# Seven block products for the last two chunk pairs of the first row group, in a linear-attention and bilinear feed-forward kernel

## The chip, the cores and the metric

The kernel runs on one core of a Trainium2 chip. The metric is the device time of one execution in microseconds. The kernel before takes 216.21 us, the median of three runs (216.19 to 216.22). The profiled execution has a span of 215.1 us; all times of single instructions below are from its start.

## The reference

Two stages, the second on the rows of the first:

```python
# attention with decay, per head, in blocks of 64 rows
intra = (q_b @ k_b.T * Dmask) @ v_b          # Dmask: lam**(i-j) for i >= j
inter = (q_b * lam**(pos+1)) @ kv_state
out_b = intra + inter
kv_state = lam**64 * kv_state + (k_b * lam**(63-pos)).T @ v_b
# bilinear feed-forward: x is (3072, 512), w_a and w_b (512, 1536), w_out (1536, 512)
out = ((x @ w_a) * (x @ w_b)) @ w_out
```

There are 4 batches, 8 heads, 768 rows a batch and 64 columns a head, so x has 512 columns. Inputs and output are float32.

## The kernel before

A **unit** is 128 rows of one batch; there are 24, and the kernel takes them in seven groups of 4, 2, 4, 4, 4, 4 and 2 units (`GROUPS`). For each unit q and k are multiplied by powers of lam (`make_qs`, `make_ks`, both L276), transposed (on TensorE by `piece_T` for units 4 to 7, by a DMA for units 8 to 23), multiplied into scores and masked (`piece_S`: TensorE L344, VectorE L361), and a running state is updated (`piece_V`). `pieces_O` makes the attention output of one or two units, transposed, as the tile xT of the group, and calls `sums`, which forms four sums and differences of xT's quarters (xs, L573 to L576).

The feed-forward part of a group follows. The 1536 inner columns are 12 chunks of 128, or 6 pairs. There are two ways to do it:

- **Directly**, in the first group (`ffn` with first set). For each chunk four matmuls make a (L518), ScalarE copies it, four make b, and VectorE multiplies the two from PSUM into ab (L545).
- **By seven block products**, in groups 1 to 6 (`ffn_seven`). x, and w_a and w_b side by side, are cut in 2 x 2 blocks, and seven products of blocks stand in for eight. The weights' sums are made once: `w_sums(i)` makes the tile tw of pair i by four VectorE subtractions (L548 to L551), t0 from the first halves of w_a and w_b, t1 and t3 also from the second. A pair takes the products in the order 1, 5, 2, 6, 3, 7, 4, mixed with those of the next pair. Product 1, then 6, 7 and 4, add up in one PSUM bank, m_q; 5 and 3 share m_r; 2 has m_p. Between them ScalarE copies s1, s5 and u2 out, and VectorE (or GpSimd) forms c11, c12 and c22 (L629 or L632, L640, L646). Product 4 adds into m_q only after VectorE has read it for c22. Two multiplications write ab: c22 by m_q on VectorE (L649), c11 by c12 on GpSimd (L642).

The output is ab @ w_out. In the first group it runs over the four units of a pair of chunks at a time (L833, `out_mms`), with other work between: after each chunk and each piece of the output a `hook(slot)` runs what `PLAN` lists for that group and slot. The slots of the first group are 0 to 11 for the chunks and 12 to 35 for the 24 pieces of the output. Groups 2 to 5 use seven block products for the output too, which need sums of w_out (`wo_sums(j)`, the tiles two, same lines as tw).

In `PLAN`, TW is w_sums, TO is wo_sums, T a transpose on TensorE, S scores and mask, V the state, O2 the attention output of two units, L loads, P both scalings of a unit, QS that of q on GpSimd, KS that of k on VectorE. Each engine works its instructions in program order, so the place in PLAN is the place in every engine's queue. GpSimd issues the loads of the weights, of v and of q and k up to unit 8; units 9 and on come over the sync engine's queue once k of unit 7 has landed (LS).

The chunks 8 to 11, pairs 4 and 5, need the last two quarters of w_a and w_b: `W_HALVES` loads them as two halves over the rows each.

Of the kernel before, what the change touches and what calls it, by code (L numbers as in the profile page):

```python
# [17 lines left out]
BF16 = mybir.dt.bfloat16  # L18
# [4 lines left out]
def _bc(ap, dims):  # L23
# [15 lines left out]


S_GROUPS = (1, 2, 3, 4, 5, 6)
SUM_ON_VEC = {1: (2,), 2: (0, 1, 2, 3, 5), 3: range(6), 4: range(6), 5: (1, 2, 4, 5), 6: (0, 1, 2)}
O_SEVEN = (2, 3, 4, 5)
O_EARLY = (5,)
ACT_COPY = (4, 10, 12, 13, 14, 16, 17, 18, 20, 21)
# [1 line left out]
W_ORDER = ("a0", "a1", "b0", "b1", "a2", "b2", "a3", "b3", "a4", "a5", "b4", "b5", "o0", "q4", "k4", "o1", "v4",  # L47
           "q5", "k5", "o2", "v5", "o3")
PLAN = {
# [21 lines left out]
def kernel(  # L71
# [47 lines left out]
    def release(i):  # L119
        bank["held"].discard(i)  # L120
        touch(i)
# [153 lines left out]
    def scale(eng, dst, x, lp):  # L275
        eng_of(eng).tensor_mul(dst.rearrange("p (c b) d -> p b c d", b=2),  # L276
                               x[:].rearrange("p (b c) d -> p b c d", b=2),
                               lp.rearrange("p (b c) o -> p b c o", b=2)
                               .to_broadcast([128, 2, HP, D]))

    def qk_of(u):
        if u not in U:
            qk = prep_pool.tile([128, 2, H, D], BF16, name="qk", tag="qk")
            U[u] = dict(qk=qk, kn=qk[:, 1])
        return U[u]["qk"]

    def make_ks(u, eng):
        scale(eng, qk_of(u)[:, 1], raw.pop((u, "k")), lp_k[:, u % NB])

    def make_qs(u, eng):  # L290
        scale(eng, qk_of(u)[:, 0], raw.pop((u, "q")), lp_q[:, u % NB])
# [252 lines left out]
        ps = half(wb_sb, f, xT, "b_ps", 0, gt)  # L544
        nc.vector.tensor_mul(ab[:, f, :gt], a_sb[:, :gt], ps[:, :gt])  # L545

    def block_sums(t, b11, b21, b12, b22):
        nc.vector.tensor_sub(t[:, 0], b12, b11)  # L548
        nc.vector.tensor_sub(t[:, 1], b22, t[:, 0])
        nc.vector.tensor_sub(t[:, 2], b22, b12)  # L550
        nc.vector.tensor_sub(t[:, 3], b21, t[:, 1])  # L551

    def w_sums(i):
        t = tw[i] = wst_pool.tile([128, 4, 2, 256], BF16, name="tw", tag="wst")
        c = slice(256 * i, 256 * i + 256)
        block_sums(t, wa_sb[:, 0:2, c], wa_sb[:, 2:4, c], wb_sb[:, 0:2, c], wb_sb[:, 2:4, c])

    def wo_block(j, k, n):
        return wo_sb[:, 4 * j + 2 * k:4 * j + 2 * k + 2, 256 * n:256 * n + 256]
# [4 lines left out]

    def sums(u):
        g = next(i for i in range(len(GROUPS)) if g_u0[i] <= u < g_u0[i] + GROUPS[i])
        if g not in S_GROUPS or u != g_u0[g] + GROUPS[g] - 1:
            return
        h = GROUPS[g] * BLK // 2
        x = xTs[u][0]  # L570
        t = wst_pool.tile([128, 4, 2, h], BF16, name="xs", tag="wst")
        x11, x12, x21, x22 = (x[:, k:k + 2, c:c + h] for c in (0, h) for k in (0, 2))
        nc.vector.tensor_add(t[:, 0], x22, x21)  # L573
        nc.vector.tensor_sub(t[:, 1], t[:, 0], x11)
        nc.vector.tensor_sub(t[:, 2], x11, x21)
        nc.vector.tensor_sub(t[:, 3], x12, t[:, 1])  # L576
        xs[g] = t

    tw, xs, two = {}, {}, {}

    def ffn_seven(g, u0, n, xT, hook, last):
        h = n * BLK // 2
        nf = 512 // h
        ab = ab_pool.tile([128, FC, 512], BF16, name="ab", tag="ab")
        st = xs.pop(g)
        live = {}

# [25 lines left out]
        def step(i, n):  # L613
            d = live.setdefault(i, {})
            if n == 1:
                d["q"], d["qb"] = bank_of("m_q")
                product(i, d["q"], w_of(wa_sb, 0, i), x11, True)
                d["s12"] = wst_pool.tile([128, 2, nf, h], F32, name="s12", tag="wst")
                snap("s1", d["q"], 0, d["s12"][:, 0])
            elif n == 5:  # L620
                d["r"], d["rb"] = bank_of("m_r")
                product(i, d["r"], t_of(0, i), st[:, 0], True)
                d["s5"] = snap("s5", d["r"], 2)
            elif n == 2:
                p, pb = bank_of("m_p")
                product(i, p, w_of(wa_sb, 2, i), x12, True)
                d["c11"] = a_pool.tile([128, nf, h], BF16, name="c11", tag="a")
                if i in SUM_ON_VEC[g]:
                    nc.vector.tensor_add(d["c11"], d["s12"][:, 0], p)  # L629
                else:  # L630
                    snap("s2", p, 0, d["s12"][:, 1])
                    nc.gpsimd.tensor_add(d["c11"], d["s12"][:, 0], d["s12"][:, 1])  # L632
                release(pb)
            elif n == 6:
                product(i, d["q"], t_of(1, i), st[:, 1], False)
                d["u2"] = snap("u2", d["q"], 1)
            elif n == 3:
                product(i, d["r"], w_of(wb_sb, 2, i), st[:, 3], False)
                c12 = sn_pool.tile([128, nf, h], F32, name="c12", tag="c12", bufs=2)
                nc.vector.tensor_add(c12, d["u2"], d["r"])  # L640
                release(d["rb"])
                nc.gpsimd.tensor_mul(ab[:, nf * i:nf * i + nf, 0:h], d["c11"], c12)  # L642
            elif n == 7:
                product(i, d["q"], t_of(2, i), st[:, 2], False)
                d["c22"] = sn_pool.tile([128, nf, h], F32, name="c22", tag="c22", bufs=1)
                nc.vector.tensor_add(d["c22"], d["s5"], d["q"])  # L646
            else:
                product(i, d["q"], t_of(3, i), x22, False)
                nc.vector.tensor_mul(ab[:, nf * i:nf * i + nf, h:2 * h], d["c22"], d["q"])  # L649
                release(d["qb"])  # L650
                live.pop(i)

        at = {}
        for i in range(FC // nf):
            for off, m in ((0, 1), (2, 5), (3, 2), (4, 6), (6, 3), (8, 7), (12, 4)):
                at[7 * i + off] = (i, m)
        end = max(at)
        for s in range(end):
            if s in at:
# [183 lines left out]
    def ffn(u0, n, xT, hook, first):  # L843
        gt = n * BLK
        ab = ab_pool.tile([128, FC, 512], BF16, name="ab", tag="ab")
        if first:
            for i, cs in enumerate(W_STEPS):
                fs = range(w_off[cs[0]] // 128, w_off[cs[-1] + 1] // 128)
                a_sbs = a_parts(fs[:2], xT, gt) if i == 0 else []
                a_sbs += [a_part(f, xT, gt) for f in fs[len(a_sbs):]]  # L850
                for n_f, (f, a_sb) in enumerate(zip(fs, a_sbs)):
                    b_part(f, xT, gt, a_sb, ab)
                    hook(f)
            ops = [ps_bank("op", [128, d_model], F32, hold=True) for _ in range(n)]
            slot = FC
            for c in range(FC // 2):
                for t in range(n):
                    out_mms(ops[t], ab, t, range(2 * c, 2 * c + 2))
                    if c == FC // 2 - 1:
                        store(u0 + t, ops[t], 0, d_model)  # L860
                    hook(slot)
                    slot += 1
            bank["held"].clear()
            return
        for f in range(FC):
            a_sb = a_part(f, xT, gt)
            b_part(f, xT, gt, a_sb, ab)
            hook(f)
        for t in range(n):
            op = ps_bank("op", [128, d_model], F32)  # L870
            out_mms(op, ab, t, range(FC // 2))
            hook(FC + 2 * t)
            out_mms(op, ab, t, range(FC // 2, FC))
            store(u0 + t, op, 0, d_model)
            hook(FC + 2 * t + 1)
# [134 lines left out]
    for g, n in enumerate(GROUPS):  # L1010
# [6 lines left out]
        def hook(slot, plan=plan):  # L1017
            for name, us in plan.get(slot, ()):
# [6 lines left out]
                elif name == "KS":  # L1025
                    make_ks(us, "dve")
                    scaled(us)
                elif name == "LS":
                    wait_for(raw[us - 2, "k"])
                    load_x("q", us, nc.sync)  # L1030
# [16 lines left out]
                    piece_T(us)  # L1047
                elif name == "SA":
                    bank["held"].update(piece_SA(us))
                elif name == "SK":  # L1050
                    bank["held"].update(piece_SK(us))
                elif name == "SM":
# [49 lines left out]
```

## Time and profile before

| stretch | us | length | TensorE busy | VectorE busy | ScalarE busy | GpSimd busy |
|---|---|---|---|---|---|---|
| chunks 8 to 11, direct | 32.12 to 39.03 | 6.91 | 6.91 | 6.67 | 2.34 | 5.74 |
| output of the first group | 39.03 to 53.78 | 14.75 | 14.75 | 10.98 | 6.95 | 11.70 |
| second group | 53.78 to 72.49 | 18.71 | 18.70 | 17.06 | 9.55 | 13.99 |
| third group | 72.49 to 104.61 | 32.12 | 32.06 | 29.15 | 17.21 | 17.15 |
| fourth group | 104.61 to 136.16 | 31.55 | 31.55 | 29.07 | 16.20 | 18.62 |

The busy columns are time with an instruction running, by the profile. For TensorE this can hide waits, since ends of matmuls are modelled; whether it waits is better read from the starts of its instructions. An instruction that waits for another engine in the middle of its work shows a greater length, not an idle time.

### The profile page before, as it was taken

Reading aid. Unit: us, or ns where it says so; the run is one execution under the profiler, and the core shown is the slowest. Engines: PE = TensorE matmul, PEld = TensorE weight load, DVE = VectorE, ACT = ScalarE, POOL = GpSimd, SP = SyncE. Lnnn points to the kernel's source line nnn. Section 1 sums busy time; section 2 is a strip of 40 time slices with the busy share of each in tenths; the row PEclk is TensorE's granted clock in tenths of the full one; section 3 lists DMA queues with packets and bytes.
Section 4 is the critical chain, followed back from the end, with each engine's and each line's share of the span. In section 5 each row is a group of like instructions: output and inputs, shape, how many; then the busy total and the mean of one; then the engine's idle time right before and its main releaser. Section 6 shows DMA issues by size and latency. Waiting matters only on the chain.

```text
span 215.1 us, 6092 instructions
## 1 busy us (share of the span) xinstructions
PE 209.1 (97%) x2491; PEld 162.9 (76%) x2491; DVE 176.4 (82%) x322; ACT 106.7 (50%) x195; POOL 125.6 (58%) x143
## 2 busy tenths in 40 slices
PE   7899999999999999999999999999999999999994
PEld 2376444455996688888888888888988888989973
DVE  0893799984997998898989998989998788996860
ACT  2587234155862565546464545555545656343621
POOL 5789577994769299920599620699700846400320
PEclk9999999999999999999999999999999999999999
DMA  3999999999999999995299992399900380002202
GB/s 101 313 145 193 200 226 227 223 222 208 130 195 175 149 194 266 169 230 102 98 155 161 262 175 38 105 173 163 251 0 3 117 154 0 3 2 95 106 0 98
DMA packets 86767, 31.32 MB, mean 146 GB/s; under 512 B 74068, under 2 KB 83156, under 8 KB 86740
## 3 DMA queue, kind: packets, MB, share of 16 engines
q1 hardware_dynamic: 53748, 20.39, 48.9%
q0 software_dynamic: 32704, 10.49, 43.0%
q8 instruction: 19, 0.31, 0.7%
q10 hardware_dynamic: 288, 0.07, 0.1%
q14 instruction: 8, 0.07, 0.1%
HBM read 28.32 MB, written 6.29 MB: 161 GB/s over the span
## 4 chain that ended last, share of the span: by engine, by line
PE 90%; DMA 3%; DVE 3%; SPq 1%; issue 1%; ACT 0%
PE m_q L595 24%; PE m_r L595 13%; PE op L833 10%; PE o_q L706 9%; PE m_p L595 6%; PE o_r L706 5%; PE a_ps L518 5%; PE b_ps L518 5%; PE o_ps L380 4%; DMA k<-in_k_dram 3%; PE kq L344 3%; PE o_p L706 2%; PE kvd L411 1%; SPq L229 1%; PE tps L321 1%; PE o_w L706 1%
## 5 line engine op out<-in xcount | busy, mean ns | idle before, releaser
L595 PEld LDWEIGHTS <-tw 128*128 128x128 bf16 x576 | 48.7, 98 | 5.4
L642 POOL TENSOR_TENSOR ab<-c,c 128x512 bf16<-128x512 bf16 x30 | 34.8, 1168 | 28.1 <-DVE c L640 27.7
L595 PE MATMUL m_q<-xs,tw 128*128 128x256 bf16 (+1 forms) x288 | 36.1, 255 | 0.0
L595 PEld LDWEIGHTS <-wa_sb 128*128 128x128 bf16 x288 | 24.7, 98 | 2.6
L610 ACT COPY s<-m_q 128x512 f32<-128x512 f32 x30 | 17.6, 588 | 17.4 <-PE m_q L595 17.3
L649 DVE TENSOR_TENSOR ab<-c,m_q 128x512 bf16<-128x512 f32 x30 | 20.5, 684 | 5.5 <-PE m_q L595 3.5
L361 DVE TENSOR_TENSOR m<-kq,lotri 128x512 bf16<-128x512 f32 x39 | 24.6, 681 | 0.2 <-PE kq L344 0.2
L298 POOL DMA_DIRECT2D vb<-in_v_dram x24 | 22.3, 934 | 1.5 <-DMA wo_sb<-in_moe_w_out_dram 1.2
L833 PE MATMUL op<-wo_sb,ab 128*128 128x512 bf16 (+2 forms) x120 | 23.1, 337 | 0.0
L640 DVE TENSOR_TENSOR c<-u,m_r 128x512 f32<-128x512 f32 x30 | 20.4, 680 | 2.3 <-ACT u L610 2.3
L610 ACT COPY s<-m_r 128x512 f32<-128x512 f32 x30 | 17.7, 589 | 9.1 <-PE m_r L595 9.1
L610 ACT COPY u<-m_q 128x512 f32<-128x512 f32 x30 | 17.7, 591 | 6.9 <-PE m_q L595 5.7
L646 DVE TENSOR_TENSOR c<-s,m_q 128x512 f32<-128x512 f32 x30 | 20.5, 685 | 0.5
L629 DVE TENSOR_TENSOR c<-s,m_p 128x512 bf16<-128x512 f32 x25 | 17.1, 685 | 4.0 <-PE m_p L595 3.6
L1040 POOL COPY gate<-xs 1x1 bf16<-1x1 bf16 x3 | 0.5, 176 | 33.8 <-DVE xs L576 33.8
L706 PEld LDWEIGHTS <-sm 128*128 128x128 bf16 x192 | 17.9, 98 | 3.0 <-DVE sm L739 0.3
L276 POOL TENSOR_TENSOR qk<-qf,lp_q 128x512 bf16<-128x512 f32 x18 | 19.3, 1072 | 0.0
L403 ACT CAST xT<-o_ps 128x512 bf16<-128x512 f32 x22 | 11.9, 588 | 12.8 <-PE o_ps L380 12.5
L595 PE MATMUL m_r<-xs,tw 128*128 128x256 bf16 (+1 forms) x144 | 18.1, 255 | 0.0
L595 PE MATMUL m_q<-xT,tw 128*128 128x256 bf16 (+1 forms) x144 | 18.1, 255 | 0.0
L595 PE MATMUL m_p<-xT,wa_sb 128*128 128x256 bf16 (+1 forms) x144 | 18.1, 255 | 0.0
L595 PE MATMUL m_q<-xT,wa_sb 128*128 128x256 bf16 (+1 forms) x144 | 18.1, 255 | 0.0
(120 smaller groups left out, 384.9 us busy)
## 6 DMA issues: line engine op xcount, KB each, us to landing
out_dram<-o_two SPq DMA_DIRECT2D x8, 512.0 KB, 2.8
qf<-in_q_dram SPq DMA_DIRECT2D x14, 256.0 KB, 5.6
kf<-in_k_dram SPq DMA_DIRECT2D x14, 256.0 KB, 6.4
vb<-in_v_dram POOLq DMA_DIRECT2D x24, 128.0 KB, 6.0
wa_sb<-in_moe_w_a_dram POOLq DMA_DIRECT2D x6, 256.0 KB, 6.9
wb_sb<-in_moe_w_b_dram POOLq DMA_DIRECT2D x6, 256.0 KB, 7.9
wo_sb<-in_moe_w_out_dram POOLq DMA_DIRECT2D x6, 256.0 KB, 8.0
out_dram<-o_kept SPq DMA_DIRECT2D x6, 256.0 KB, 5.2
```

What stands on the lines that cost most here:

```text
L276: eng_of(eng).tensor_mul(dst.rearrange("p (c b) d -> p b c d", b=2), x[:].rearrange("p (b c) d -> p b c d", b=2), lp.rearrange("p (b c) o ...
L298: nc.gpsimd.dma_start(out=vb, in_=vr[b, nb])
L361: nc.vector.tensor_mul(m, kq[i], lotri_bc)
L518: nc.tensor.matmul(ps[:, lo:hi], lhsT=w_sb[:, s, f * 128:(f + 1) * 128], rhs=xT[:, s, lo:hi], start=(s == 0), stop=(s == KS - 1), skip_gro ...
L595: nc.tensor.matmul(ps[:, f, :], lhsT=w(k, f), rhs=x[:, k, :], start=(first and f == 0 and k == 0), stop=True, skip_group_check=True)
L610: nc.scalar.copy(t, ps)
L640: nc.vector.tensor_add(c12, d["u2"], d["r"])
L642: nc.gpsimd.tensor_mul(ab[:, nf * i:nf * i + nf, 0:h], d["c11"], c12)
L646: nc.vector.tensor_add(d["c22"], d["s5"], d["q"])
L649: nc.vector.tensor_mul(ab[:, nf * i:nf * i + nf, h:2 * h], d["c22"], d["q"])
L706: nc.tensor.matmul(ps[:, t, :], lhsT=x(j, c)[:, t * BLK:(t + 1) * BLK], rhs=w(j)[:, c, :], start=(first and t == 0 and j == js[0] and c == ...
L833: nc.tensor.matmul(op[:, lo:hi], lhsT=ab[:, f, t * 128:(t + 1) * 128], rhs=wo_sb[:, f, lo:hi], start=(f == 0), stop=(f == FC - 1))
```

## The change

In the first group chunks 0 to 7 stay direct. Pairs 4 and 5 are made by seven block products, with the code of the later groups, cut into `pair_plan` and `pair_steps`. What it needs comes earlier: the sums of the first group's own x (XS, in slot -1, before the first chunk), and tw of pairs 4 and 5. tw3 moves back, behind the scores of unit 5. c11 is added on VectorE for both pairs, and c11 by c12 is on VectorE in this group. The last product 4 of pair 5 comes after the seventh piece of the output. The scaling of k of units 4 to 6 leaves VectorE: ScalarE does it head by head, in four parts of two heads (KA). The sums two0 move from slot 16 to 32 of the first group, and two1 from the start of the third group to slot 35 of the first. It is for fewer columns on TensorE.

```diff
+S_PAIRS = (4, 5)
+PAIR_SLOTS = {1: 8, 4: 9, 8: 10, 11: 11, 13: 11.3, 15: 11.6}
+SUM_ON_VEC = {0: S_PAIRS, 1: (2,), 2: (0, 1, 2, 3, 5), 3: range(6), 4: range(6), 5: (1, 2, 4, 5), 6: (0, 1, 2)}
...
-    0: [(0, "V", 3), (1, "TW", 0), (3, "TW", 1), (5, "TW", 2), (7, "TW", 3), (7, "TW", 4),
-        (9, "P", 4), (9, "L", ("q6", "k6", "o4")), (11, "P", 5), (11, "L", ("q7", "k7", "o5")),
-        (12, "L", ("v6", "v7")), (14, "T", 4), (16, "TO", 0), (17, "S", 4), (17, "P", 6), (18, "T", 5),
-        (18, "L", ("q8", "k8", "v8")), (21, "V", 4), (22, "S", 5), (22, "LS", 9), (23, "P", 7), (23, "QS", 8),
-        (23, "L", ("v9",)), (24, "T", 6), (26, "O2", (4, 5)), (28, "S", 6), (29, "T", 7), (29, "KS", 8),
-        (30, "QS", 9), (31, "TW", 5)],
+    0: [(-1, "XS", 3), (-1, "TW", 0), (0, "V", 3), (1, "TW", 1), (3, "TW", 2), (5, "TW", 4), (7, "TA", 5), (10, "TB", 5),
+        (9, "L", ("q6", "k6", "o4")), (11, "QS", 4), (11, "L", ("q7",)), (11, "QS", 5), (11, "L", ("k7", "o5")),
+        (11, "KA", (4, 0)), (11.3, "KA", (4, 1)), (11.6, "KA", (4, 2)), (12, "KA", (4, 3)),
+        (16, "KA", (5, 0)), (17, "KA", (5, 1)), (18, "KA", (5, 2)), (19, "KA", (5, 3)),
+        (12, "L", ("v6", "v7")), (14, "T", 4), (17, "QS", 6), (18, "S", 4), (18, "L", ("q8", "k8", "v8")), (20, "T", 5),
+        (21, "V", 4), (22, "LS", 9), (22, "KA", (6, 0)), (23, "S", 5), (23, "KA", (6, 1)), (24, "KA", (6, 2)),
+        (24, "KA", (6, 3)), (24, "TW", 3), (25, "P", 7), (25, "QS", 8), (25, "L", ("v9",)), (26, "O2", (4, 5)),
+        (28, "T", 6), (31, "S", 6), (32, "TO", 0), (33, "T", 7), (33, "KS", 8), (34, "QS", 9), (35, "TO", 1)],
...
-    2: [(0, "TO", 1), (0, "TO", 2), (0, "GT", None), (1, "P", 12), (4, "P", 13), (7, "P", 14), (10, "S", 10), (11, "S", 11),
+    2: [(0, "TO", 2), (0, "GT", None), (1, "P", 12), (4, "P", 13), (7, "P", 14), (10, "S", 10), (11, "S", 11),
...
+    def make_ks_part(u, part):
+        x = raw[u, "k"]
+        for h in range(2 * part, 2 * part + 2):
+            c, b = divmod(h, 2)
+            nc.scalar.activation(qk_of(u)[:, 1, h, :], x[:, 4 * b + c, :], AF.Copy,
+                                 scale=lp_k[:, u % NB, 4 * b + c, :])
...
-                nc.gpsimd.tensor_mul(ab[:, nf * i:nf * i + nf, 0:h], d["c11"], c12)
+                if g > 0:
+                    nc.gpsimd.tensor_mul(ab[:, nf * i:nf * i + nf, 0:h], d["c11"], c12)
+                d["c12"] = c12
...
                 nc.vector.tensor_mul(ab[:, nf * i:nf * i + nf, h:2 * h], d["c22"], d["q"])
+                if g == 0:
+                    nc.vector.tensor_mul(ab[:, nf * i:nf * i + nf, 0:h], d["c11"], d["c12"])
...
         if first:
-            for i, cs in enumerate(W_STEPS):
+            hook(-1)
+            nf, step = pair_steps(0, n, xT, ab)
+            for i, cs in enumerate(W_STEPS[:-1]):
...
+            at = pair_plan(S_PAIRS)
+            end = max(at)
+            for s in range(end):
+                if s in at:
+                    step(*at[s])
+                if s in PAIR_SLOTS:
+                    hook(PAIR_SLOTS[s])
...
+                    if slot == FC + 6:
+                        step(*at[end])
```

TA and TB call `w_sums` for its first and its last two subtractions; XS calls `sums`.

More of the change, by code (lines that the diff above doesn't have):

```diff
@@ L41 @@
 S_GROUPS = (1, 2, 3, 4, 5, 6)
-SUM_ON_VEC = {1: (2,), 2: (0, 1, 2, 3, 5), 3: range(6), 4: range(6), 5: (1, 2, 4, 5), 6: (0, 1, 2)}
+S_PAIRS = (4, 5)
+PAIR_SLOTS = {1: 8, 4: 9, 8: 10, 11: 11, 13: 11.3, 15: 11.6}
+SUM_ON_VEC = {0: S_PAIRS, 1: (2,), 2: (0, 1, 2, 3, 5), 3: range(6), 4: range(6), 5: (1, 2, 4, 5), 6: (0, 1, 2)}
 O_SEVEN = (2, 3, 4, 5)
@@ L288, in make_ks @@
         scale(eng, qk_of(u)[:, 1], raw.pop((u, "k")), lp_k[:, u % NB])
+    def make_ks_part(u, part):
[4 more added lines that the diff above has]
+                                 scale=lp_k[:, u % NB, 4 * b + c, :])
+        if part == 3:
+            raw.pop((u, "k"))
+            scaled(u)
     def make_qs(u, eng):
@@ L545, in b_part, with block_sums, w_sums @@
         nc.vector.tensor_mul(ab[:, f, :gt], a_sb[:, :gt], ps[:, :gt])
[L547 to L554, printed above, removed]
+    def block_sums(t, b11, b21, b12, b22, parts=(0, 1)):
+        if 0 in parts:
+            nc.vector.tensor_sub(t[:, 0], b12, b11)
+            nc.vector.tensor_sub(t[:, 1], b22, t[:, 0])
+        if 1 in parts:
+            nc.vector.tensor_sub(t[:, 2], b22, b12)
+            nc.vector.tensor_sub(t[:, 3], b21, t[:, 1])
+    def w_sums(i, parts=(0, 1)):
+        if 0 in parts:
+            tw[i] = wst_pool.tile([128, 4, 2, 256], BF16, name="tw", tag="wst")
         c = slice(256 * i, 256 * i + 256)
-        block_sums(t, wa_sb[:, 0:2, c], wa_sb[:, 2:4, c], wb_sb[:, 0:2, c], wb_sb[:, 2:4, c])
+        block_sums(tw[i], wa_sb[:, 0:2, c], wa_sb[:, 2:4, c], wb_sb[:, 0:2, c], wb_sb[:, 2:4, c], parts)
     def wo_block(j, k, n):
@@ L566, in sums @@
         g = next(i for i in range(len(GROUPS)) if g_u0[i] <= u < g_u0[i] + GROUPS[i])
-        if g not in S_GROUPS or u != g_u0[g] + GROUPS[g] - 1:
+        if g not in (0,) + S_GROUPS or u != g_u0[g] + GROUPS[g] - 1:
             return
@@ L579, with pair_plan, pair_steps @@
     tw, xs, two = {}, {}, {}
-    def ffn_seven(g, u0, n, xT, hook, last):
+    def pair_plan(pairs):
+        return {7 * k + off: (i, m) for k, i in enumerate(pairs)
+                for off, m in ((0, 1), (2, 5), (3, 2), (4, 6), (6, 3), (8, 7), (12, 4))}
+    def pair_steps(g, n, xT, ab):
         h = n * BLK // 2
         nf = 512 // h
-        ab = ab_pool.tile([128, FC, 512], BF16, name="ab", tag="ab")
         st = xs.pop(g)
@@ L649, in step, with ffn_seven @@
                 nc.vector.tensor_mul(ab[:, nf * i:nf * i + nf, h:2 * h], d["c22"], d["q"])
+                if g == 0:
+                    nc.vector.tensor_mul(ab[:, nf * i:nf * i + nf, 0:h], d["c11"], d["c12"])
                 release(d["qb"])
                 live.pop(i)
[L653 to L656, printed above, removed]
+        return nf, step
+    def ffn_seven(g, u0, n, xT, hook, last):
+        ab = ab_pool.tile([128, FC, 512], BF16, name="ab", tag="ab")
+        nf, step = pair_steps(g, n, xT, ab)
+        at = pair_plan(range(FC // nf))
         end = max(at)
@@ L1027, in hook @@
                     scaled(us)
+                elif name == "KA":
+                    make_ks_part(*us)
                 elif name == "LS":
@@ L1049, in hook @@
                     bank["held"].update(piece_SA(us))
+                elif name == "TA":
+                    w_sums(us, (0,))
+                elif name == "TB":
+                    w_sums(us, (1,))
+                elif name == "XS":
+                    sums(us)
                 elif name == "SK":
```

## The prediction

> **What bounds the kernel now.** I read the page first: TensorE is never short of work. Then the timeline of VectorE, GpSimd and TensorE where the first group hands over to the second, because the change fills the first group's end with VectorE work.
>
> ```profile
> PE 209.1 (97%) x2491; PEld 162.9 (76%) x2491; DVE 176.4 (82%) x322; ACT 106.7 (50%) x195; POOL 125.6 (58%) x143
> PE   7899999999999999999999999999999999999994
> ```
>
> TensorE sets the time: 97% busy, every slice from the third to the last but one at 9. A TensorE saving counts in full, unless TensorE then waits for another engine. The timeline (start, length, instruction):
>
> ```profile
> 50.92 1.28 DVE L361 TENSOR_TENSOR m<-kq,lotri 128x512 bf16<-128x512 f32 x2
> 52.35 1.04 POOL L276 TENSOR_TENSOR qk<-qkf,lp_q 128x512 bf16<-128x512 f32 x1 [3.05 <-DMA qkf<-in_q_dram]
> 53.63 0.69 DVE L276 TENSOR_TENSOR qk<-qkf,lp_k 128x512 bf16<-128x512 f32 x1 [1.44 <-DMA qkf<-in_k_dram]
> 54.24 0.42 DVE L548 TENSOR_TENSOR tw<-wb_sb,wa_sb 128x512 bf16<-128x512 bf16 x1
> ...
> 55.37 0.42 DVE L551 TENSOR_TENSOR tw<-wa_sb,tw 128x512 bf16<-128x512 bf16 x1
> 55.42 1.27 POOL L276 TENSOR_TENSOR qk<-qkf,lp_q 128x512 bf16<-128x512 f32 x1 [1.14 <-DMA qkf<-in_q_dram]
> 55.71 0.68 DVE L444 TENSOR_TENSOR st<-kvd,bdiag 128x512 bf16<-128x512 f32 x1
> 56.39 0.84 DVE L276 TENSOR_TENSOR qk<-qkf,lp_k 128x512 bf16<-128x512 f32 x1
> 56.66 1.72 POOL L632 TENSOR_TENSOR c<-s 128x512 bf16<-128x512 f32 x1
> 57.16 0.68 DVE L473 TENSOR_TENSOR m<-kq,lotri 128x512 bf16<-128x512 f32 x1
> 57.76 0.67 DVE L640 TENSOR_TENSOR c<-u,m_r 128x512 f32<-128x512 f32 x1
> 58.35 0.67 DVE L646 TENSOR_TENSOR c<-s,m_q 128x512 f32<-128x512 f32 x1
> 59.08 0.61 PE L595 MATMUL m_q<-xT,tw 128*128 128x128 bf16 x8
> ```
>
> Three readings. VectorE idles 1.44 us before 53.63, waiting for k of unit 8. From there to 59.02 it has no gap. The last VectorE row, c22 of the second group's first pair, must have read m_q before product 4 adds into that bank; it ends at 59.02, product 4 starts at 59.08, and product 6 before it started at 58.48 and takes 0.45 (two such products take 0.89 in the chain of waits). So TensorE already waits about 0.15 us here: **this hand-over is VectorE's**.
>
> The other thing to see is what happens when GpSimd and VectorE both work out of SBUF:
>
> ```profile
> 34.91 1.72 DVE L549 TENSOR_TENSOR tw<-wb_sb,tw 128x512 bf16<-128x512 bf16 x1
> 35.28 1.06 POOL L276 TENSOR_TENSOR qk<-qf,lp_q 128x512 bf16<-128x512 f32 x1
> ```
>
> L549 has a median of 0.424 us; beside this GpSimd multiply it took 1.72, 1.30 more.
>
> **What the Trainium skill says.** "SBUF — State Buffer", section "SBUF: two separate sides": GpSimd and VectorE share one port pair, and a VectorE instruction with two SBUF inputs and a GpSimd instruction that reads SBUF exclude each other for a whole instruction. The trace agrees: the 1.72 above. The same page, "Who interferes with whom", says that VectorE with one SBUF input is free of this; L640 beside GpSimd multiplies at 75.49 took 0.68, its usual time. "ScalarE: Activation LUTs", "What ACT_TABLE_LOAD costs": an ACTIVATE takes 186 ns + 0.833 ns an element, 93 more for a pointer operand, and neighbours overlap by 93. Without the pointer this gives 252.6 ns at 80 columns; L260 took 252. The trace has no such instruction with a pointer scale.
>
> **The change, part by part.**
>
> *Fewer TensorE columns.* Out go 32 matmuls of 512 columns, 32.12 to 39.03 = 6.91 us (0.216 each). In come 14 products of four 256-column matmuls; eight such matmuls take 0.87 in the chain of waits, so 14 x 0.437 = 6.12. **Saved 0.79 us.**
>
> *A new wait inside it.* Product 4 of pair 4 needs VectorE's c22. GpSimd's wait at 31.78 shows the last half of w_b landing then. VectorE does after it: three tw4 sums at their spacing of 0.34 (1.02), two b_part products at 0.60 (1.20), two tw5 sums (0.79), c11, c12 (1.20) and c22 (0.68): 31.82 + 4.89 = 36.71. TensorE comes there at 32.12 + 10 x 0.437 = 36.49. **Lost 0.27.** Behind it stand product 3 of pair 5 and the output matmuls, so it is on the path.
>
> *Sums of x and tw0 moved ahead.* Eight bf16 sums, about 3 us, fall in VectorE's 3.99 us idle before 22.66: nothing. The ten VectorE operations on the products replace four b_part products and three scalings of k; between 40 and 47 us VectorE has pauses (7.70 of 10 us busy) for the difference.
>
> *k of units 4 to 6 on ScalarE.* Eight 64-column ACTIVATEs a unit. Bounds: 0.17 each, the spacing of L259 and L260, and 0.332, the skill's price without overlap; I take 0.24, so 1.9 us a unit (1.4 to 2.7). Unit 4 starts after the last u2 at 37.2 and ends at 39.1; its transpose on TensorE comes after six output matmuls at about 39.4. Units 5 and 6 fall into ScalarE's waits (10 us of it are 3.24 to 4.84 busy here). Nothing, or 0.5 at the upper price. The GpSimd queue holds the same instructions, two scalings of q a few places later, so k of unit 8 is still asked for at about 46.0 and lands at 53.6.
>
> So TensorE would end the first group at 53.78 - 0.79 + 0.27 = 53.26.
>
> *The hand-over.* VectorE's order there becomes: masks of unit 6, **two0 (4 sums), k of unit 8, two1 (4 sums)**, state, k of unit 9, mask, c12, c22. Unit 6's scores now end eight output matmuls and a transpose before the group's end: 8 x 0.216 + 0.45 = 2.18, at 51.08. From there 1.20 + 1.47 + 0.61 + 1.47 + 0.64 + 0.69 + 0.60 + 0.60 + 0.68 = 7.96, and c22 ends at about 59.1. Without a stall in the first group it would be 58.9. **The 0.52 us are gone here in either case**, since two0 fills the 1.44 us that were idle: about +0.1 against 59.02. Everything on TensorE behind product 4 waits along.
>
> *The port.* In that idle time q of unit 8 was scaled on GpSimd (52.35 to 53.39). q lands when it did (asked for at 45.06), and now meets two0: VectorE stands still for about that multiply, 1.0 us. k of unit 8 ends near 55.4, and two1 then meets q of unit 9 (55.42) and GpSimd's sum c11 (ready near 56.4), 1.0 and 1.2 us if VectorE loses both. In the kernel before, VectorE lost only 0.15 at 56.39, as state, which reads one SBUF operand, ran meanwhile. I take one lost multiply: **+1.0**.
>
> *Four sums fewer at the start of group 2.* VectorE catches up by 79.8 (0.26 idle) and TensorE doesn't wait there: nothing.
>
> Sum: 216.21 + 0.1 + 1.0 = **217.3**, taken as 217.2 because the scores may come 0.1 early.
>
> **Rivals.**
> - *The saving survives* (faster): 216.21 - 0.79 + 0.27 = 215.7, or 215.4 with no new wait. For it: TensorE is the bound on the page. Against it: VectorE's unbroken chain to 59.02.
> - *VectorE just keeps pace* (no change): q of unit 8 lands while the masks run, or GpSimd waits and runs beside state. 216.0 to 216.6. For it: at 47.77 a GpSimd multiply took 1.54 beside VectorE's 0.69, so VectorE can win. Against it: q landed at 52.3, just as the masks would end.
> - *All collide* (slower): 1.0 + 1.0 + 1.2 and the 0.1: up to 219.5; with two of them 218.3. For it: the later VectorE gets, the more of GpSimd's queue it meets.
>
> **How the numbers follow.** One collision 0.34 (216.8 to 217.8), more 0.24, keeps pace 0.22, saving survives 0.20. The range takes in the likeliest, the even case, the lesser half of the survivors, and the two-collision time: 215.6 to 218.4. Faster 0.20, same 0.22, slower 0.58.
>
> **What would show it.** Right: m_q (product 4 of pair 4) on TensorE waits 0.2 to 0.5 near 36.5; the first group ends near 53.3; VectorE's two sums at 52 to 57 show one of over 1 us beside a GpSimd multiply; product 4 of the second group's first pair starts near 60.2 behind c22, and later groups keep their lengths (32.12 and 31.55 for the next two). Wrong: that product starts before 58.7, or the second group is shorter than 18.7 us.

## The result and the profile after

The changed kernel takes **218.45 us** (median of five, 218.08 to 220.04) against 216.21 (215.96 to 216.34): the ratio is 1.0129, with a 95% interval of 1.0089 to 1.0169. It is slower by 2.24 us. The ratio of the two medians alone is 1.0104: two of the five executions, at 219.85 and 220.04, stand apart (without them the median is 218.26), and the last section comes back to them. The profiled execution took 218.08, 1.87 above the median of before. The profiled execution of before took 216.77, 0.56 above its median, and it comes to chunk 8 later (32.12) than the changed kernel comes to its first block product (31.64). Where that point lies varies from one execution to another: in the run "two1 alone" below, which up to there is the kernel before, chunk 8 starts at 31.46. So stretches are compared by length, counted from these two starts.

The page of the changed kernel, engines and TensorE's slices:

```profile
PE 208.4 (96%) x2515; PEld 165.4 (76%) x2515; DVE 181.3 (84%) x329; ACT 113.7 (53%) x221; POOL 124.5 (58%) x143
PE   7899999999789999999999999999999999999994
```

TensorE is busy for 0.7 us less than before, and yet the kernel is slower. The row of slices says where: the eleventh and twelfth slice (each 5.4 us, so from 54 to 65 us) are at 7 and 8 where they were 9. That is the hand-over from the first group to the second. The same stretch in the timeline of VectorE (start, length, instruction, idle time before it and what ended it):

```profile
46.99 1.33 DVE L564 TENSOR_TENSOR tw<-wb_sb,tw 128x512 bf16<-128x512 bf16 x1
...
50.45 1.28 DVE L375 TENSOR_TENSOR m<-kq,lotri 128x512 bf16<-128x512 f32 x2
51.65 0.42 DVE L563 TENSOR_TENSOR two<-wo_sb 128x512 bf16<-128x512 bf16 x1
...
53.11 0.69 DVE L280 TENSOR_TENSOR qk<-qkf,lp_k 128x512 bf16<-128x512 f32 x1
53.71 0.42 DVE L563 TENSOR_TENSOR two<-wo_sb 128x512 bf16<-128x512 bf16 x1
54.16 1.15 DVE L564 TENSOR_TENSOR two<-wo_sb,two 128x512 bf16<-128x512 bf16 x1
55.23 0.41 DVE L566 TENSOR_TENSOR two<-wo_sb 128x512 bf16<-128x512 bf16 x1
55.57 1.49 DVE L567 TENSOR_TENSOR two<-wo_sb,two 128x512 bf16<-128x512 bf16 x1
56.98 0.68 DVE L458 TENSOR_TENSOR st<-kvd,bdiag 128x512 bf16<-128x512 f32 x1
...
59.38 0.67 DVE L668 TENSOR_TENSOR c<-s,m_q 128x512 f32<-128x512 f32 x1
```

and that of GpSimd:

```profile
50.52 1.04 POOL L280 TENSOR_TENSOR qk<-qkf,lp_q 128x512 bf16<-128x512 f32 x1 [2.49 <-DMA qkf<-in_q_dram]
...
53.74 1.29 POOL L280 TENSOR_TENSOR qk<-qkf,lp_q 128x512 bf16<-128x512 f32 x1 [1.29 <-DMA qkf<-in_q_dram]
55.49 1.28 POOL L652 TENSOR_TENSOR c<-s 128x512 bf16<-128x512 f32 x1 [0.46 <-ACT s L630]
```

Read the two side by side. VectorE's row has no gap from the masks of unit 6 (50.45) to 60.05, but two of the four sums two1 are too long. L564 starts at 54.16 and the next instruction 1.07 us later, where two0 shows 0.34: 0.73 lost, beside GpSimd's q of unit 9 (53.74). L567 holds its place for 1.41 instead of 0.34: 1.07 lost, beside GpSimd's sum c11 (55.49). Together that is **1.80 us**. The multiply of q of unit 8, which the prediction priced, ran at 50.52 beside the masks, which read one operand from PSUM, and cost nothing: two0 is four sums of usual length. An earlier meeting cost TensorE nothing, for another reason: at 46.99 a sum of tw3, which the change moved there, lost 0.92 beside a GpSimd multiply (46.94, 1.09 long), but the masks at 50.45 had to wait in any case for the scores of unit 6, which start on TensorE at 49.98. In the kernel before, masks that VectorE stood waiting for began 0.45 after their scores (45.44 and 45.89).

TensorE, early in that chain and at its end:

```profile
54.49 0.61 PE L615 MATMUL m_q<-xs,tw 128*128 128x128 bf16 x8 [0.24 <-ACT s L630]
...
57.62 0.61 PE L615 MATMUL m_q<-xs,tw 128*128 128x128 bf16 x8
60.10 0.61 PE L615 MATMUL m_q<-xT,tw 128*128 128x128 bf16 x8 [1.87 <-DVE c L668]
```

Product 6 of the second pair starts at 57.62 and takes 0.45, so TensorE stands from 58.07 until c22 is there at 60.05: 2.0 us. Without the 1.80 lost c22 would have ended at 58.25, and the stand would be 0.2.

The account, in lengths:

| stretch | before | after | difference |
|---|---|---|---|
| chunk 8 (first block product) to the second group's start | 21.66 | 20.88 | -0.78 |
| from there to product 4 of its first pair | 5.30 | 7.58 | +2.28 |
| product 4 to the third group's start | 13.41 | 13.63 | +0.22 |
| third and fourth group | 32.12, 31.55 | 32.20, 31.54 | +0.07 |

The sum is +1.79, against the 1.87 between the profiled execution and the median of before. The +2.28 are 1.88 of waiting more for c22 (2.03, from 58.07 to 60.10, against 0.15 before) and 0.40 that TensorE spends more ahead of it. These 0.40 stand before product 6 of the first pair (54.49): it starts 0.86 after the product ahead of it, 0.44 before, and the profile shows 0.24 of this as idle time. By the profile it waits for ScalarE's first copy s of the second group, which comes 1.28 us after the group's start, 0.82 before. Ahead of it in ScalarE's row the copy of the transposed q and k of unit 7 (51.94 to 52.97) now comes later, with two copies of the output behind it. No run puts that copy back, so that it is the reason is read from the row and not shown by an experiment.

### The profile page after: what moved, and what is told of

It is laid out like the page before. It is cut to its first block, busy times and chain, and to the rows that moved or that the text cites. A ratio compares the mean times of both kernels' runs of the same rounds, so it can differ in the third digit from the quotient of the medians.

```text
span 216.4 us, 6175 instructions
## 1 busy us (share of the span) xinstructions
PE 208.4 (96%) x2515; PEld 165.4 (76%) x2515; DVE 181.3 (84%) x329; ACT 113.7 (53%) x221; POOL 124.5 (58%) x143
## 4 chain that ended last, share of the span: by engine, by line
PE 64%; DMA 13%; POOL 10%; DVE 5%; issue 2%; SPq 2%; ACT 1%; POOLq 0%
PE m_q L615 22%; PE m_r L615 11%; PE o_q L732 9%; PE m_p L615 5%; PE o_r L732 5%; DMA wo_sb<-in_moe_w_out_dram 5%; PE op L859 4%; DMA k<-in_k_dram 3%; DMA qkf<-in_k_dram 3%; POOL qk L280 2%; DMA kf<-in_k_dram 2%; PE o_ps L394 2%; PE kq L358 2%; PE o_p L732 2%; POOL wa_sb L177 1%
## 5 line engine op out<-in xcount | busy, mean ns | idle before, releaser
L615 PEld LDWEIGHTS <-tw 128*128 128x128 bf16 x608 | 51.9, 98 | 8.3 <-issue 2.4
L615 PE MATMUL m_q<-xs,tw 128*128 128x256 bf16 (+1 forms) x304 | 38.5, 256 | 0.2 <-ACT s L630 0.2
L630 ACT COPY s<-m_q 128x512 f32<-128x512 f32 x32 | 18.8, 589 | 19.9 <-PE m_q L615 19.8
L615 PEld LDWEIGHTS <-wa_sb 128*128 128x128 bf16 x304 | 26.3, 98 | 3.0
L671 DVE TENSOR_TENSOR ab<-c,m_q 128x512 bf16<-128x512 f32 x32 | 21.9, 685 | 6.7 <-PE m_q L615 4.8
L660 DVE TENSOR_TENSOR c<-u,m_r 128x512 f32<-128x512 f32 x32 | 21.8, 682 | 2.6 <-ACT u L630 2.3
L630 ACT COPY s<-m_r 128x512 f32<-128x512 f32 x32 | 18.9, 591 | 9.3 <-PE m_r L615 8.5
L668 DVE TENSOR_TENSOR c<-s,m_q 128x512 f32<-128x512 f32 x32 | 21.9, 685 | 0.4
L649 DVE TENSOR_TENSOR c<-s,m_p 128x512 bf16<-128x512 f32 x27 | 18.5, 686 | 4.2 <-PE m_p L615 3.9
L615 PE MATMUL m_r<-xs,wb_sb 128*128 128x256 bf16 (+1 forms) x152 | 19.3, 256 | 0.0
```

Source lines behind the costliest of these rows:

```text
L615: nc.tensor.matmul(ps[:, f, :], lhsT=w(k, f), rhs=x[:, k, :], start=(first and f == 0 and k == 0), stop=True, skip_group_check=True)
L630: nc.scalar.copy(t, ps)
```

## The experiments

All were run in five rounds beside the kernel before. Three theories on the loss were on trial. **P**: the sums two1 in the hand-over are lengthened by GpSimd's instructions. **L**: only the number of VectorE's instructions in the hand-over counts, four sums or 1.47 us. **S**: the block products in the first group cost the time themselves, and the sums two1 matter little. A fourth, **C**, is on the spread of the times: the executions near 220 us come from the stand of TensorE.

### two1 back in the third group

The changed kernel, with these two edits:

```diff
-        (28, "T", 6), (31, "S", 6), (32, "TO", 0), (33, "T", 7), (33, "KS", 8), (34, "QS", 9), (35, "TO", 1)],
+        (28, "T", 6), (31, "S", 6), (32, "TO", 0), (33, "T", 7), (33, "KS", 8), (34, "QS", 9)],
-    2: [(0, "TO", 2), (0, "GT", None), ...
+    2: [(0, "TO", 1), (0, "TO", 2), (0, "GT", None), ...
```

> The changed kernel with one edit undone: two1 goes back to the start of group 2. Theory P (port): in the changed kernel two of the four two1 sums on VectorE lost 0.73 and 1.07 us to GpSimd multiplies; c22 of the second group's first pair ended at 60.05 and TensorE stood 1.87 us. Without two1 VectorE's stretch from 53.71 to 56.98 (3.27 us) is gone, c22 ends near 56.8, TensorE, which is ready at 58.07, waits for nothing: 2.0 us less than the changed kernel, 215.3 to 216.2, so at or below the kernel before. Theory L (only the number of VectorE instructions counts): the same sign, but 1.5 us less, near 217. Theory S (the seven products in the first group cost the time themselves, by waits or by the clock): it stays near 218.4.

Measured: **216.35**, ratio 1.0000 (0.9982 to 1.0019). The loss of 2.1 us is gone with these four sums, which S doesn't allow, and it is more than L's 1.5. VectorE and TensorE at the hand-over:

```profile
54.67 0.69 DVE L280 TENSOR_TENSOR qk<-qkf,lp_k 128x512 bf16<-128x512 f32 x1 [0.29 <-DMA qkf<-in_k_dram]
...
56.85 0.69 DVE L668 TENSOR_TENSOR c<-s,m_q 128x512 f32<-128x512 f32 x1
...
57.99 0.61 PE L615 MATMUL m_q<-xT,tw 128*128 128x128 bf16 x8
```

VectorE has an idle 0.29 before k of unit 9 again, c22 ends at 57.54, and product 4 follows product 6 (57.54, 0.45) without a wait: 26.43 us after the first block product, against 26.96 before. So 0.53 us of the columns saved do arrive. That the kernel is still no faster is told by the start of the third group, where all eight sums of w_out stand in a row, as in the kernel before:

```profile
68.81 1.04 DVE L590 TENSOR_TENSOR xs<-xT 128x512 bf16<-128x512 bf16 x1 [1.08 <-ACT xT L417]
...
71.50 0.42 DVE L563 TENSOR_TENSOR two<-wo_sb 128x512 bf16<-128x512 bf16 x1
...
74.09 0.42 DVE L567 TENSOR_TENSOR two<-wo_sb,two 128x512 bf16<-128x512 bf16 x1
...
75.62 0.68 DVE L668 TENSOR_TENSOR c<-s,m_q 128x512 f32<-128x512 f32 x1
...
76.36 0.60 PE L615 MATMUL m_q<-xT,tw 128*128 128x256 bf16 x4 [0.35 <-DVE c L668]
```

TensorE got there 0.5 us earlier and waits for c22, 0.35 us as idle time and 0.51 by the starts of its products. That wait took a meeting as well: the sum xs ahead of them lost 0.62 beside a GpSimd multiply (68.52). Without that loss c22 would have ended at 75.68, and TensorE was ready at 75.85, so the eight sums alone would just have kept pace. Counted from the first block product this product starts after 44.80 us; from chunk 8 in the kernel before it starts after 44.81. The saving is spent.

### two1 alone, in the kernel before

```diff
-        (30, "QS", 9), (31, "TW", 5)],
+        (30, "QS", 9), (31, "TW", 5), (35, "TO", 1)],
-    2: [(0, "TO", 1), (0, "TO", 2), (0, "GT", None), ...
+    2: [(0, "TO", 2), (0, "GT", None), ...
```

> The kernel before with one part of the change alone: two1 moved from the start of group 2 to the end of group 1 (slot 35), nothing else. Theory P: VectorE's unbroken chain there (53.63 to 59.02) takes four sums more, 1.47 us, and these meet q of unit 9 and c11 on GpSimd, 0.7 to 1.1 us each: c22 ends at 61.5 to 62.5, and the time is 218.5 to 219.7. Theory L: 1.5 us more, 217.7. Theory S: two1 is harmless, 216.2 to 216.5.

Measured: **218.61**, ratio 1.0115 (1.0072 to 1.0159). The four sums cost 2.4 us without a single block product in the first group, so S falls. All six executions, 218.19 and more, lie above the 217.7 of L. VectorE and GpSimd in this kernel, whose line numbers are those of the kernel before:

```profile
54.25 1.29 DVE L551 TENSOR_TENSOR tw<-wa_sb,tw 128x512 bf16<-128x512 bf16 x1
...
55.91 1.38 DVE L549 TENSOR_TENSOR two<-wo_sb,two 128x512 bf16<-128x512 bf16 x1
...
60.27 0.68 DVE L646 TENSOR_TENSOR c<-s,m_q 128x512 f32<-128x512 f32 x1
```

```profile
54.22 1.03 POOL L276 TENSOR_TENSOR qk<-qkf,lp_q 128x512 bf16<-128x512 f32 x1 [1.02 <-DMA qkf<-in_q_dram]
55.62 1.39 POOL L632 TENSOR_TENSOR c<-s 128x512 bf16<-128x512 f32 x1 [0.37 <-ACT s L610]
```

The same two partners each meet one sum: q of unit 9 the last sum of tw5 (0.87 lost), c11 one of two1 (0.96). In this execution only the second is owed to the move: with four more sums in the queue VectorE is still in sums when c11 comes; without them it was at state and k of unit 9. That q of unit 9 meets tw5 is a matter of its landing, 1.11 us after the second group's start here and 1.64 in the profile of before. Landing at 1.64 here, at 54.75, it would have met two1, which without lost time runs from 54.59 to 56.06.

### c11 on VectorE

The changed kernel, with GpSimd's sum taken out of the way:

```diff
-SUM_ON_VEC = {0: S_PAIRS, 1: (2,), ...
+SUM_ON_VEC = {0: S_PAIRS, 1: (0, 2), ...
```

> The changed kernel with c11 of the second group's first pair on VectorE and not on GpSimd, so that one of the two collisions has no partner. Theory P: VectorE gets back 1.07 us at two1's last sum and pays 0.60 us for c11: product 4 starts near 59.6 and the time is 0.5 us less, 217.9. Theory L: one VectorE instruction more in the chain, 0.6 us more, 219.0. Theory S: 218.4.

Measured: **217.41**, ratio 1.0056 (1.0036 to 1.0076), 1.0 us less than the changed kernel although VectorE has one instruction more; P had put 0.5 less, L 0.6 more. VectorE in it:

```profile
54.28 1.15 DVE L564 TENSOR_TENSOR two<-wo_sb,two 128x512 bf16<-128x512 bf16 x1
...
55.69 0.41 DVE L567 TENSOR_TENSOR two<-wo_sb,two 128x512 bf16<-128x512 bf16 x1
```

L567 is back at 0.41, and L564, whose partner is untouched, is still at 1.15. That names c11 as the partner of L567.

### q of unit 9 behind two1

The changed kernel, with the other partner moved: GT makes GpSimd wait until the sums two1 are written, and holds back q of unit 9 and, behind it, c11.

```diff
-(33, "KS", 8), (34, "QS", 9), (35, "TO", 1)],
+(33, "KS", 8), (35, "TO", 1), (35, "GT", None), (35, "QS", 9)],
```

> The changed kernel with GpSimd's multiply for q of unit 9 (and with it all behind it on GpSimd, c11 first) held back until two1 is done, by the one-element copy that group 2 uses for the same end. VectorE has the same instructions in the same order. Theory P: two1 loses nothing (1.80 us back); k of unit 9 may wait up to 0.5 for the multiply that now starts with the state copy; c22 ends at 58.3 to 58.8, TensorE waits 0.2 to 0.7: 1.3 to 1.8 us less than the changed kernel, near 217.0. Theory L and theory S: nothing changes, 218.4.

Measured: **217.22**, ratio 1.0036 (1.0018 to 1.0055), 1.2 us less than the changed kernel, with the same instructions on VectorE; P had put 217.0, L and S no difference. In the profiled execution all four sums two1 are at 0.42 or 0.43, and the multiply meets k of unit 9 instead:

```profile
57.37 1.28 DVE L280 TENSOR_TENSOR qk<-qkf,lp_k 128x512 bf16<-128x512 f32 x1
```

A collision moved is not a collision removed: 0.6 us are lost here. This execution took 218.58, far from its median, for reasons ahead of the hand-over: its first block product started at 32.14, 0.5 later than in the changed kernel's profile, and w_b's last half was used first at 32.67 (30.86 there), so product 4 of pair 4 waited:

```profile
37.61 0.60 PE L615 MATMUL m_q<-xT,tw 128*128 128x256 bf16 x4 [0.77 <-DVE c L668]
```

That is the wait that the prediction put at 0.27 and that the changed kernel's own profile lacks. It depends on a landing that varies between executions.

### two1 in the kernel before, before k of unit 8

```diff
-(28, "S", 6), (29, "T", 7), (29, "KS", 8),
+(28, "S", 6), (28, "TO", 1), (29, "T", 7), (29, "KS", 8),
-    2: [(0, "TO", 1), (0, "TO", 2), (0, "GT", None), ...
+    2: [(0, "TO", 2), (0, "GT", None), ...
```

> The kernel before with two1 moved to slot 28 of the first group, between the masks of unit 6 and k of unit 8, where VectorE waited 1.44 us for k of unit 8 (0.97 in the profile with two1 alone). No seven products in the first group. Theory P: the sums fill idle time, and lose at most one GpSimd multiply: 216.2 to 217.0, no gain, since TensorE's work is the same. Theory L (four more VectorE instructions cost their 1.47 us): 217.7. If it were faster than the kernel before, the gain of two1 in slot 32 would be the move and not the seven products.

Measured: **217.75**, ratio 1.0071 (1.0046 to 1.0097). I had expected 216.2 to 217.0, since VectorE idles there; this missed, and the time is the 217.7 that L had put. The trace of this run doesn't bear L out. The sums two1 themselves ran at 0.42 where VectorE had idled; k of unit 8 comes behind them at 53.31, and what follows it then met GpSimd:

```profile
54.36 1.15 DVE L549 TENSOR_TENSOR tw<-wb_sb,tw 128x512 bf16<-128x512 bf16 x1
...
56.71 1.16 DVE L276 TENSOR_TENSOR qk<-qkf,lp_k 128x512 bf16<-128x512 f32 x1
```

```profile
53.99 1.24 POOL L276 TENSOR_TENSOR qk<-qkf,lp_q 128x512 bf16<-128x512 f32 x1 [1.26 <-DVE qk L276]
...
56.02 1.30 POOL L632 TENSOR_TENSOR c<-s 128x512 bf16<-128x512 f32 x1 [0.79 <-ACT s L610]
```

A sum of tw5 lost 0.74 beside q of unit 9, and k of unit 9 lost 0.48 beside c11. c22 ended at 59.67; without these 1.22 it would have ended at 58.45, and TensorE was ready for product 4 at 58.66. It doesn't matter which sums are in the chain.

### Both sums of w_out early

The changed kernel with two0 back at slot 16, where VectorE stood 1.25 us ahead of product 4 of pair 5, and two1 in two0's place at slot 32, so that the hand-over holds four sums of w_out instead of eight and the third group starts with four:

```diff
-        (12, "L", ("v6", "v7")), (14, "T", 4), (17, "QS", 6), ...
+        (12, "L", ("v6", "v7")), (14, "T", 4), (16, "TO", 0), (17, "QS", 6), ...
-(32, "TO", 0), (33, "T", 7), (33, "KS", 8), (34, "QS", 9), (35, "TO", 1)],
+(32, "TO", 1), (33, "T", 7), (33, "KS", 8), (34, "QS", 9)],
```

> The changed kernel with two0 in slot 16 (where VectorE stood 1.25 us before product 4 of pair 5, and GpSimd only issued loads) and two1 in slot 32, where two0 was; the hand-over then has four sums as with two1 taken back, and group 2 begins with four and not eight. With two1 back at group 2, TensorE still waited 0.35 us on TensorE's own row and 0.5 on its weight row for c22 of group 2's first pair, behind eight sums. Theory P (it is where VectorE's sums lie that spends the saving): both waits gone, 0.5 us less than with two1 taken back: 215.5 to 215.9, faster than the kernel before. Theory S (the seven products themselves give nothing once the rest is mended): 216.2 to 216.4.

Measured: **215.88**, ratio 0.9987 (0.9976 to 0.9998): faster than both kernels, by 0.3 us than the one before, which is just clear of the noise. S had put 216.2 to 216.4. VectorE and TensorE at its hand-over:

```profile
55.10 0.76 DVE L280 TENSOR_TENSOR qk<-qkf,lp_k 128x512 bf16<-128x512 f32 x1
...
57.29 0.69 DVE L668 TENSOR_TENSOR c<-s,m_q 128x512 f32<-128x512 f32 x1
...
58.43 0.61 PE L615 MATMUL m_q<-xT,tw 128*128 128x128 bf16 x8
```

c22 ends at 57.98, 0.45 before product 4. The waits of TensorE from 45 to 75 us (engine, line, what it waited for: total us, times, longest):

```profile
PE op L859 <- issue: 0.3, 2, 0.2
PE m_q L615 <- ACT s L630: 0.2, 1, 0.2
```

No wait for c22 in either group. What keeps it from the whole 0.79: its second group starts 21.30 us after the first block product, 20.88 in the changed kernel, and the wait for ScalarE's copy s is there as well, 0.2 as idle time and 0.41 by the starts.

### The changed kernel again, and its wait filled

Two of the five executions of the changed kernel were near 220 us at a mean granted clock of 0.992, the rest at 0.998 to 1.0. The first of these runs repeats the changed kernel unedited. The second gives TensorE eight matmuls into a bank of their own, which nothing reads, before product 4 of that pair:

```diff
+                if g == 1 and i == 0:
+                    fill = ps_bank("fill", [128, 512], F32)
+                    for _ in range(8):
+                        nc.tensor.matmul(fill, lhsT=ident, rhs=wa_sb[:, 0, 0:512], ...
```

> The changed kernel again, on the chip of the next runs, as their base. 218.1 to 218.5 where the granted clock is 1.0, and about 219.9 in the runs with 0.992 (two of five before).

> The changed kernel with eight matmuls of 512 columns into an unused PSUM bank (1.7 us of TensorE work that nobody reads) ahead of product 4 of the second group's first pair, where TensorE stands 1.87 us. Theory C (the runs with a clock of 0.992 come from this stand of TensorE): no run with 0.992 any more, times of 218.0 to 218.4, hardly any near 220. Rival (the clock has another cause): as many runs near 220 as without the filling. Either way the runs at clock 1.0 stay where they were, within 0.2.

Measured: **218.49** again (1.0115, 1.0089 to 1.0142), with L564 at 1.15, L567 at 1.49 and product 4 waiting 2.0 us as before, one of six executions at 0.992; and **218.65** with the fill (1.0113, 1.0092 to 1.0135), none of six. TensorE in the second (the trace has seven of the eight):

```profile
59.02 1.89 PE L673 MATMUL fill<-wa_sb,ident 128*128 128x512 bf16 x7 [0.69 <-DVE m L487]
60.74 0.61 PE L615 MATMUL m_q<-xT,tw 128*128 128x128 bf16 x8
```

The fill waited 0.69 us for its bank and then took the place of the rest of the wait; the time is the changed kernel's within the interval, and not the 218.0 to 218.4 of C. On the clock it decides nothing by counts: 3 of 11 executions against 0 of 6 is what chance could give. Nor is the clock all of the spread: one execution of each of the two runs took longer, 219.29 and 219.67, at a clock of 1.0.

## Why the prediction was wrong

The direction and the mechanism were right (slower, by sums meeting GpSimd in the hand-over); the size was not: +1.0 forecast, +2.24 measured, just above the range. By its steps:

- **Saved 0.79 on TensorE: right.** 13 of the 14 products ran from 31.64 to 37.33, 0.438 each, and the second group started 0.78 sooner.
- **Lost 0.27 at product 4 of pair 4: not in this profile.** The product started at 36.02 on time, because w_b's half was there about 0.5 us earlier against TensorE's work: VectorE's first use of it is at 30.86, 0.78 before the first block product, where 0.3 was assumed. The wait exists (0.77 in the one execution above) but not in every one.
- **k on ScalarE at 0.24 each, hidden: right.** Eight ACTIVATEs of unit 4 took 2.02 us (from 36.70), 0.25 each, between the two bounds, of which the upper came from the Trainium skill, "ScalarE: Activation LUTs", "What ACT_TABLE_LOAD costs". No wait on TensorE is put down to it. VectorE's added operations cost TensorE nothing there either, though the forecast misread its pauses: the 7.70 of 10 us busy are from 40 to 50, and from 40 to 47 VectorE is busy for 6.80 of 7. What the forecast had at nothing on ScalarE is the wait for its first copy s in the second group: 0.40 on TensorE.
- **"I take one lost multiply: +1.0": the step that failed.** It is the term of the sum that was mis-sized, and its partner was wrong. I let q of unit 8 meet two0, because it was scaled at 52.35 before, and "q lands when it did" didn't hold: asked for at 44.23 (45.06 before), it was there 6.3 us later and not 7.3. It came at 50.52 and met the masks, at no cost. The two meetings that I listed as possible, two1 with q of unit 9 and with c11, both took place, 0.73 and 1.07: 1.80 in place of 1.0. The rival "all collide" had put two at 218.3, and that is what was measured but for 0.15.
- **"The 0.52 us are gone here in either case": too strong.** The chain alone, without lost time, would end at 58.25 for a TensorE that is ready at 58.07. It takes 7.80 from the masks' start, against 7.96 in the forecast (whose own sum ends at 59.04, so +0.02 and not +0.1). With four sums fewer in it (two1 back, and both sums early) TensorE doesn't wait for c22 at all.
- **Four sums fewer in the third group, nothing: right only for a TensorE that comes late.** With two1 back in its place and TensorE 0.5 us earlier, the eight sums and a lost 0.62 at xs end in a wait of 0.35.
- **Later groups keep 32.12 and 31.55: right**, 32.20 and 31.54. The second group took another 0.22 behind product 4, which was not forecast.

The rival that the saving survives fell with VectorE's chain, as the prediction said. What told between one collision and two could have been read in the trace of before: c11 stood there at 56.66 beside state and k, just behind the last sum. Four sums more, 1.47 us, had to bring a sum under it. And k of unit 8 was to end near 55.4 by the prediction, which is when q of unit 9 landed (55.42).

## What to carry to other kernels

When VectorE gets more work with two SBUF operands, lay the partner's instructions under the *new* places of VectorE's queue one by one, and price each meeting at 0.5 to 1.1 us (the hand-overs here; 1.3 in one place of the kernel before), not the sum's own 0.34. Work taken off the bound is worth nothing past the first place where another engine has no slack; move sums to where that engine pauses before shortening the bound. A move that fills an idle gap also moves everything behind the gap, and that may then collide, as two1 before k of unit 8 did.

## What the runs showed of the hardware

- In the hand-over a meeting costs VectorE less than the GpSimd instruction beside it takes by the profile (1.03 to 1.39 us): 0.73 and 1.07 in the changed kernel, 0.87 and 0.96 in two1 alone, 0.74 and 0.48 in two1 before k of unit 8, 0.60 with q of unit 9 behind two1. The Trainium skill, "SBUF — State Buffer", "SBUF: two separate sides", says that the two exclude each other for a whole instruction; the trace agrees in kind, with these smaller sums. VectorE's row shows one long instruction and no idle time. How much of a meeting GpSimd's row shows varies: q of unit 9 meets a sum in the changed kernel, in its repeat and in two1 alone, and is 1.29, 1.12 and 1.03 long there; it is 1.03 in two1 back, where it meets none.
- A stand of TensorE can perhaps be paid twice. Executions at a mean granted clock of 0.991 to 0.992 took 1.6 to 2 us more than the median of the rest of their kernel. They came in the changed kernel (3 of 11), two1 alone (2 of 6) and c11 on VectorE (2 of 22), in all of which TensorE stands over 1.3 us in the hand-over (in the last in two parts, 0.57 and 0.74 as idle time). They came in none of the 22 of q of unit 9 behind two1, with a stand of 0.67, and in none of the 86 executions of the kernel before that ran beside the experiments. The profiled one of two1 alone shows it, by stretches (TensorE's busy time stands first behind the length; the clock granted to it is the third figure from the end):

```profile
55.00:58.50 3.50, 3.42 (x70) 3.11 (x67) 3.47 (x7) 2.56 (x6) 1.64 (x2) 1.00 0.91 83
58.50:61.00 2.50, 0.00 (x0) 0.00 (x0) 2.50 (x6) 0.69 (x2) 0.50 (x1) 1.00 0.24 45
61.00:62.00 1.00, 0.99 (x14) 0.99 (x14) 0.91 (x2) 0.03 (x1) 1.00 (x2) 0.75 0.82 149
62.00:63.00 1.00, 1.00 (x13) 1.00 (x10) 0.77 (x2) 0.00 (x0) 0.89 (x1) 0.50 0.42 98
...
65.00:66.00 1.00, 1.00 (x29) 0.90 (x30) 0.42 (x1) 0.63 (x2) 0.03 (x1) 1.00 1.43 233
```

After the stand, 2.6 us of idle time, TensorE runs at half its clock from about 61.5 to 64.9; a product starts every 0.85 us in place of 0.45. Half of 3.4 us is 1.7 us, the size of the difference. The Trainium skill, "TensorE: Matmul & The Clock Gate", "What's actually happening", says that the clock is halved after an idle window of about 3.4 us whose place in time is not tied to the kernel. Half the clock for about that long is what the trace shows; the stand before it was shorter than such a window, and it had this sequel in some executions only. That the stand is its cause fits all of this, but it isn't shown: the run with the filled wait had too few executions.
